# Block 0's attention fully by seven products, its matrix sums made earlier and sent through DRAM, and small steps reordered in a linear-attention + MLP kernel

## The chip, the cores and the metric

The kernel runs on one core of one Trainium2 chip. The metric is the time of one execution on the device in microseconds (us). Before the change it is 408.38 us, the median of three runs (408.17 to 408.54).

## The reference

```python
xn = layernorm(x)                                   # x: 2048 tokens x 512
qkv = xn @ wqkv                                     # 32 heads of 16
pq, pk = phi(q), phi(k)                             # phi(t) = (t+1 if t>0 else exp(t)) + 1e-6
kv = einsum("bhsd,bhse->bhde", pk, v); z = sum_s pk
o = (pq @ kv) / (pq . z + 1e-6)                     # per head
attention = o @ wo
h = relu(xn @ w1 + b1) ** 2                         # 512 -> 1376
out = x + attention + h @ w2 + b2
```

All is float32. What matters here: `kv` and `wo` are folded into one 512x512 matrix M, so that attention of a token is (weighted phi(q)) @ M.

## The kernel before, in words

**Precision.** Every matrix product is done on split numbers: a high part (float32r) and a low part (the rest). `three` (L130) and `PASSES` make one product from three matmuls: high*high, high*low, low*high. A split costs an ACT copy for the high part (`copy`, L114) and a DVE subtraction for the low part (`rest_of`, L125, or `split`, L122).

**Tiling.** 2048 tokens are four blocks of 512, and a block is four tiles of 128 tokens. A first stage normalises all tokens, makes keys and the matrix M; M's raw form goes to DRAM as `md`. Then a loop `for n in range(2)` takes the blocks in two pairs: blocks 3 and 2 (n=0), then blocks 1 and 0 (n=1). t1 is the first block of the pair, t2 the second.

**A pair's passes.** For each pair, passes p = 0 to 6 (NO = 7) make two 128-column chunks of q or of the MLP's hidden layer for both blocks at once, with Strassen's scheme: seven products of six matmuls instead of eight. Kinds by pass: q, w, q, w, w, w, w. They are written into four PSUM banks: A and `before` (banks 0 and 1, which change places from pass to pass), B (bank 2) and C (bank 3). On PE the order in a pass is: `A12`-type products into A and B, S1 into C, then the product `A22b` with `T[4]` into the bank `before` of the pass ahead, second-layer sums of the MLP (`mlp_2`, L501), then S2 into A, S4 into C, perhaps a second `mlp_2`, then S3 into A.

The product with `T[4]` is the place to watch. It adds onto the bank `before`, while that bank still holds the last pass's A, which is needed alone: at the start of the next pass DVE adds it to a saved value (L1184, `t5 = before + t5`). So PE cannot start the T[4] product until that DVE addition is done. In the trace this product is the second half of a row `b<-T,aop` of twelve matmuls, whose first half is S1. In names such as `t5_1_3`, `c12_1_3`, `c11_1_6` the first number is n and the second the pass that made it.

After the passes comes p = NO, a shorter one: `mlp_2`, the T[4] product, then block 1's attention by seven products (`Seven`), mixed with more `mlp_2`. Then block 0's MLP: nine `mlp_2` of twelve matmuls (e = 0 to 8), attention of block 0, the sums of the last two hidden chunks, and the stores.

**Seven.** `class Seven` (L972) does a block's attention product (512 tokens x 512) @ M by Winograd's seven quarter products instead of eight. It needs four sums over the block (`sums_o`, DVE, L986), four of M (`sums_m`), and the high and low parts of both sums (`parts_o`, `parts_m`). `run` (L1019, matmuls at L1028) issues six matmuls of 256 columns for one tile pair `e`; `into` (L1031, L1036) adds a PSUM half bank into the result in SBUF on DVE. `x` and `y` are the PSUM tiles that are shared by several quarters.

Before the change, block 1 goes through the full seven (both tile pairs, e = 0, 1). Block 0 uses `half = Seven(t2, (0,))` (L1476): tiles 0 and 2 by seven products, tiles 1 and 3 by `add_attention` (24 matmuls of 512 columns, L133). M is loaded again from `md` in pass 6 on SP's queue (`load_m`), its sums and parts are made by DVE and ACT in pass 6 and the pass after it.

**What sets the order.** Each engine executes its own instructions in the order in which the code issues them. Apart from the fixed order of the passes there are small steps of attention, queued in `steps[t1]` and `steps[t2]` (from `steps_of`, L421: phi, weighted, sums, quotients, divide, into_parts, for one of four chunks j of q). `step(k)` takes k of them out. Two hand-written tables say how many are taken where: `AT` (a row per pass, a column for each of nine places in the pass) and `AE` (one number for each e of block 0's MLP).

Of the kernel before, what the change touches and what calls it, by code (L numbers as in the profile page):

```python
# [18 lines left out]
def kernel(  # L19
# [401 lines left out]
    def steps_of(t, j, done=False, parts=False):  # L421


        o = q[t][:, j]
        tiles = []
        blocks = lambda ap: ap.rearrange("p (r c) -> p r c", c=32)
        heads_of = lambda ap: ap.rearrange("p (h d) -> p h d", h=H)
        by_heads = lambda ap: ap.rearrange("p (r h) d -> p r h d", h=2)

        def weighted():  # L430
            pz = w512(f"pz{t}_{j}", "p", 6)
            tiles.append(pz)
            nc.scalar.activation(pz, o, AF.Identity, bias=zc[:, 1, j:j + 1], scale=zc[:, 0, j:j + 1])

        def sums():
            pt = w512(f"pt{t}_{j}", "p", 6)
            den = small.tile([P, H], F32, name=f"dt{t}_{j}", tag="den")
            nc.vector.transpose(blocks(pt), blocks(tiles[0]))
            nc.vector.tensor_reduce(den, heads_of(pt), axis=AX.X, op=OP.add)  # L439
            tiles.append(den)  # L440

        def quotients():
            pz, den = tiles
            nc.vector.tensor_scalar(den, den, 1e-6, None, op0=OP.add)
            nc.vector.reciprocal(den, den)
            nc.vector.transpose(by_heads(heads_of(pz)), by_heads(den[:, :, None].to_broadcast([P, H, D // H])))

        def divide():
            nc.vector.scalar_tensor_tensor(o, o, 1e-6, tiles[0], op0=OP.add, op1=OP.mult)
# [519 lines left out]

    LO, HI = slice(0, D // 2), slice(D // 2, D)  # L970

    class Seven:  # L972
# [15 lines left out]
        def load_m(self):  # L988
            self.mt = both("mt", ("xs0h", "xs0l"))
            self.raw = four("mraw", "B0", pool=keep)  # L990
            nc.sync.dma_start(self.raw, md)
            self.m = [[self.raw[:, 2 * r:2 * r + 2, c] for c in (LO, HI)] for r in range(2)]

        def sums_m(self):

            (b11, b12), (b21, b22) = self.m
            return [lambda: self.op(b11, b12, b11, OP.subtract), lambda: self.op(b12, b22, b12, OP.subtract),
                    lambda: self.op(b22, b22, b11, OP.subtract), lambda: self.op(b21, b21, b22, OP.subtract)]
# [15 lines left out]

        def parts_m(self):

            return self.parts(self.raw, self.mt, ((1, HI), (0, HI), (0, LO), (1, LO)))
# [24 lines left out]
    for n in range(2):  # L1042
# [128 lines left out]
        for p in range(NO + 1):  # L1171
# [21 lines left out]
            if n and p == NO:  # L1193
                step()
                do(sums, 2)
                highs_m, lows_m = seven.parts_m()
            step(at_p[7] - (n and p == NO))
            if n and p == NO:
                do(highs_m, 2)
                do(sums)  # L1200
                do(highs_m, 2)
            if (kind, fa) == ("w", 2):
                next_2(2)
            if kind:
# [16 lines left out]
                step(at_p[0])  # L1221
            if kind:
# [36 lines left out]
            if n and p == NO - 1:  # L1259
                do(sums)  # L1260
                sums = seven.sums_m()
# [18 lines left out]
            if n and p == NO - 1:  # L1280
                do(sums)
            step(at_p[2])
            if p + 1 < NO:
# [9 lines left out]
            step(at_p[3])  # L1293
            if p == NO - 1 and n:
                do(bias, 2)
# [11 lines left out]
            step(at_p[4])  # L1307
            if n == 0 and p == 0:
# [11 lines left out]
            step(at_p[5])  # L1320
            if n and p == NO - 1:
# [16 lines left out]
            step(at_p[6])  # L1338
            if n == 0 and p == 0:
# [46 lines left out]
        if n:  # L1386
# [9 lines left out]
            do(lows_m, 4)  # L1396
# [46 lines left out]
        for e, f in enumerate(waiting[:-2]):  # L1443
            mlp_2(acc, f, s.pop(f))
# [43 lines left out]
        if n:  # L1488
            xh, yh = (bank(f"{w}h", "acc")[:, LO] for w in "xy")
            half.run(xh, ("a", 0, 0), ("m", 0, LO), 0, True)  # L1490
            half.run(acc[0][:, LO], ("a", 1, 0), ("m", 1, LO), 0)
            half.run(acc[2][:, LO], ("a", 1, 1), ("t", 1, LO), 0)
            half.into(xh, 0, LO)
            for f in reversed(last_two):
                wait_for(f)
            add_attention(acc, t2 * TB + 1)
            add_attention(acc, t2 * TB + last, True)
            half.run(acc[0][:, HI], ("s", 1, 0), ("m", 1, HI), 0)
            half.run(xh, ("s", 0, 0), ("t", 1, HI), 0)
            half.run(yh, ("s", 0, 1), ("t", 0, HI), 0, True)  # L1500
            half.into(xh, 2, LO)
            half.run(xh, ("s", 1, 1), ("t", 0, LO), 0)
            half.into(yh, 2, ALL)
            for k in (0, 2):
                half.into(xh, k, HI)
# [54 lines left out]
```

## Time and profile before

| what | before |
|---|---|
| median of three runs | 408.38 us |
| the profiled execution's own time | 408.15 us |
| its span on the core | 406.4 us |
| PE (matmuls) busy | 401.5 us, 99% of the span |
| DVE busy | 326.7 us, 80% |
| ACT busy | 274.0 us, 67% |
| POOL busy | 49.7 us, 12% |
| mean granted TensorE clock | 0.999 |

The profiled execution lies 1.75 us outside its span (start and end of the program) and 0.23 us below the median. A row of the timeline reads: start us, duration us, engine, line, operation, out<-in by the program's names without numbers, partitions x elements, count, and in brackets the engine's idle time just before with what ended it. A name like `b` or `t` stands for many tiles. PE's matmuls overlap, so the distance between starts tells their pace, not the duration. Second-pair passes start on PE at 253.7 (p=0), and block 0's attention at 387.5 us.

### The profile page before, as it was taken

Reading aid. Unit: us, or ns where it says so; the run is one execution under the profiler, and the core shown is the slowest. Engines: PE = TensorE matmul, PEld = TensorE weight load, DVE = VectorE, ACT = ScalarE, POOL = GpSimd, SP = SyncE. Lnnn points to the kernel's source line nnn. Section 1 sums busy time; section 2 is a strip of 40 time slices with the busy share of each in tenths; the row PEclk is TensorE's granted clock in tenths of the full one; section 3 lists DMA queues with packets and bytes.
Section 4 is the critical chain, followed back from the end, with each engine's and each line's share of the span. In section 5 each row is a group of like instructions: output and inputs, shape, how many; then the busy total and the mean of one; then the engine's idle time right before and its main releaser. Section 6 shows DMA issues by size and latency. Waiting matters only on the chain.

```text
span 406.4 us, 5813 instructions
## 1 busy us (share of the span) xinstructions
PE 401.5 (99%) x1993; PEld 333.1 (82%) x1993; DVE 326.7 (80%) x598; ACT 274.0 (67%) x478; POOL 49.7 (12%) x81
## 2 busy tenths in 40 slices
PE   8999999999999999999999999999999999999996
PEld 7788888888788888888878888888888888888885
DVE  5886667587898999988349997567989688999885
ACT  5677777556888788886818751677587859848440
POOL 5443333220000000030000300000000200000300
PEclk9999999999999999999999999999999999999999
DMA  5856657910563231381564912412221856015612
GB/s 213 278 168 223 208 158 205 257 29 0 130 184 80 77 103 27 105 214 19 202 232 131 209 33 101 118 53 52 52 79 32 229 103 232 2 52 202 110 26 103
DMA packets 47550, 51.10 MB, mean 126 GB/s; under 512 B 8417, under 2 KB 31201, under 8 KB 47138
## 3 DMA queue, kind: packets, MB, share of 16 engines
q1 hardware_dynamic: 45138, 46.55, 37.0%
q0 software_dynamic: 2304, 4.20, 6.4%
q8 instruction: 15, 0.25, 0.2%
q14 instruction: 13, 0.11, 0.1%
q10 hardware_dynamic: 80, 0.00, 0.0%
HBM read 38.81 MB, written 10.75 MB: 122 GB/s over the span
## 4 chain that ended last, share of the span: by engine, by line
PE 97%; DMA 1%; DVE 1%; ACT 0%; issue 0%
PE acc L133 33%; PE b L497 33%; PE pk L378 11%; PE kx L398 11%; PE acc L508 2%; PE acc L1028 2%; PE pz L133 1%; PE x L1028 1%; DMA x<-in_A_x_dram 1%; PE b L133 1%; PE pz0b L133 1%; PE xh L1028 1%; PE y L1028 0%; PE acc L515 0%; PE pt L310 0%; DVE st L236 0%
## 5 line engine op out<-in xcount | busy, mean ns | idle before, releaser
L133 PE MATMUL acc<-w2r,s 128*128 128x512 f32 x477 | 113.0, 390 | 0.0
L133 PEld LDWEIGHTS acc<-w2r,s 128*128 128x128 f32 x477 | 89.2, 188 | 19.1 <-issue 0.7
L497 PE MATMUL b<-T,aop 128*128 128x512 f32 x336 | 83.5, 389 | 0.0
L497 PEld LDWEIGHTS b<-T,aop 128*128 128x128 f32 x336 | 63.0, 188 | 13.9 <-ACT t L114 0.8
L1147 POOL DMA_DIRECT2D res<-in_B_b_dram x16 | 14.4, 1042 | 277.8 <-DVE dt L439 91.0
L398 PE MATMUL kx<-pk,tok 128*128 128x512 f32 x192 | 46.0, 389 | 0.0
L398 PEld LDWEIGHTS kx<-pk,tok 128*128 128x128 f32 x192 | 36.0, 188 | 7.6 <-ACT pk L114 0.2
L497 PE MATMUL b<-xs0h,aop 128*128 128x512 f32 x112 | 36.9, 390 | 0.0
L114 ACT ACTIVATE aop<-S 128x512 fp32r<-128x512 f32 x28 | 17.5, 624 | 12.5 <-DVE S L735 12.5
L359 POOL TENSOR_TENSOR tok<-xp,tok 128x512 fp32r<-128x512 f32 x15 | 20.2, 1344 | 39.7 <-ACT tok L114 39.7
L497 PEld LDWEIGHTS b<-xs0h,aop 128*128 128x128 f32 x112 | 21.0, 188 | 4.4
L125 DVE TENSOR_TENSOR w2r<-r,w2r 128x512 fp32r<-128x512 f32 (+2 forms) x35 | 23.7, 681 | 0.5 <-ACT w2r L114 0.4
L114 ACT ACTIVATE w2r<-r 128x512 fp32r<-128x512 f32 x32 | 19.6, 619 | 6.4 <-PE acc L133 5.5
L122 DVE TENSOR_TENSOR aop<-S,aop 128x512 fp32r<-128x512 f32 x28 | 19.2, 687 | 4.8 <-ACT aop L114 4.4
L497 PE MATMUL b<-xs0l,aop 128*128 128x512 f32 x56 | 21.8, 389 | 0.0
L133 PE MATMUL acc<-mh,aTsr 128*128 128x512 f32 x64 | 20.7, 389 | 0.0
L122 DVE TENSOR_TENSOR s<-c,s 128x512 fp32r<-128x512 f32 x20 | 13.5, 688 | 8.7 <-ACT s L114 8.6
L497 PE MATMUL b<-xs1h,aop 128*128 128x512 f32 x56 | 19.5, 389 | 0.0
L114 ACT ACTIVATE T<-Tf 128x512 fp32r<-128x512 f32 x16 | 9.5, 624 | 14.4 <-DVE Tf L678 14.3
L114 ACT ACTIVATE c<-b 128x512 f32<-128x512 f32 x28 | 16.4, 587 | 2.6 <-PE b L497 2.4
L369 ACT ACTIVATE k<-pk 128x512 f32<-128x512 f32 x16 | 9.4, 590 | 9.9 <-PE pk L378 9.8
L114 ACT ACTIVATE pk<-k 128x512 fp32r<-128x512 f32 x16 | 10.1, 631 | 8.6 <-DVE k L373 8.5
(259 smaller groups left out, 828.3 us busy)
## 6 DMA issues: line engine op xcount, KB each, us to landing
r<-in_B_w_dram SPq DMA_DIRECT2D x49, 256.0 KB, 3.5
res<-in_A_x_dram SPq DMA_DIRECT2D x8, 512.0 KB, 4.7
res<-in_B_b_dram POOLq DMA_DIRECT2D x16, 256.0 KB, 5.8
out_dram<-res SPq DMA_DIRECT2D x15, 256.0 KB, 2.2
via<-xp SPq DMA_DIRECT2D x5, 512.0 KB, 2.8
xg<-via SPq DMA_DIRECT2D x20, 128.0 KB, 2.8
xTd<-t SPq DMA_DIRECT2D x8, 256.0 KB, 4.1
x<-in_A_x_dram SPq DMA_DIRECT2D x4, 512.0 KB, 4.1
```

Source lines behind the costliest of these rows:

```text
L114: nc.scalar.activation(o, i, AF.Copy, bias=bias)
L122: ENG[el].tensor_tensor(out=l, in0=src, in1=f32(h), op=OP.subtract)
L125: nc.vector.tensor_tensor(out=l, in0=src, in1=f32(h), op=OP.subtract)
L133: nc.tensor.matmul(ps, lhsT=a[u], rhs=b[v], start=first and n == 0, stop=last and n == 2)
L359: ENG[el].tensor_tensor(out=l, in0=src, in1=f32(h), op=OP.subtract)
L369: nc.scalar.activation(p, ps, AF.Relu, scale=-1.0)
L378: nc.tensor.matmul(ps, lhsT=cols(i)[u][:, j, slot(i)], rhs=w[v][:, j, :], start=first and n == 0, stop=last and n == len(steps) - 1)
L398: nc.tensor.matmul(kxp[c], lhsT=tok[i][:, u, c * P:(c + 1) * P], rhs=pk[i][:, v], start=i == 0 and (u, v) == first, stop=i == NT - 1 and ( ...
L497: nc.tensor.matmul(ps, lhsT=a[u][:, j * P:(j + 1) * P], rhs=b[v][:, j, :], start=first and j == 0 and n == 0, stop=last and j == 1 and n == 2,
L508: nc.tensor.matmul(ps, lhsT=s[u][:, k * P:(k + 1) * P], rhs=w2s[NF - 1][u][:, a:z], start=first and u == 0, stop=stop and u == 1)
L1028: nc.tensor.matmul(ps, lhsT=a, rhs=b, start=first and i == 0 and n == 0, stop=False, skip_group_check=True)
L1147: nc.gpsimd.dma_start(r[:, i], b2[None, :].partition_broadcast(P), accum_op=OP.add)
```

## The change

Three things change, all for n = 1.

1. Block 0's attention goes through the full `Seven` (`half = Seven(t2)`): 84 matmuls of 256 columns in place of 42 of them and 24 of 512 columns. The last `mlp_2` before it (e = 8, hidden chunk 1) is moved behind it. For chunks j < 2 of blocks 0 and 1, only the half of the tokens that `Seven` reads is split (`into_parts`).
2. M's sums are made by a new function, `matrix_sums`: POOL's queue loads `md` into two tiles `mr0`, `mr1` at the start of n = 1; DVE makes four subtractions at place 0 of pass 1; four `parts` (an ACT copy into a tile `mh`, a DVE subtraction in place, and two POOL DMAs of 128x2x256 that store high and low parts to DRAM) are taken at places 5 and 6 of pass 1 and of pass 3. `load_m` then loads the finished parts on POOL's queue (two transfers of 1 MB) in pass 6, and the work on M in passes 6 and 7 is gone, as is SP's load of `md`.
3. The tables: `AT`'s last two rows, `AE`, and `step(3)` in place of the low parts of M take block 0's small steps earlier.

```diff
-            split(a[:, 0], a[:, 1], o, "act", "dve")
+            used = BT // 2 if t < NB // 2 and j < 2 else BT
+            split(a[:, 0, :used], a[:, 1, :used], o[:, :used], "act", "dve")
...
+    def matrix_sums():
+        t = [two(f"mr{r}") for r in range(2)]
+        for r in range(2):
+            nc.gpsimd.dma_start(t[r], md[:, 2 * r:2 * r + 2])
+        def op(o, x, y):
+            return lambda: nc.vector.tensor_tensor(out=o, in0=x, in1=y, op=OP.subtract)
+        def parts(r, at):
+            x, to = t[r][:, :, at], slice(2 * r, 2 * r + 2)
+            h = work.tile([P, 512], F32R, name=f"mh{r}{at.start}", tag="p", bufs=6).rearrange("p (j n) -> p j n", j=2)
+            copy("act", h, x)
+            rest_of(x.bitcast(F32R), x, h)
+            nc.gpsimd.dma_start(mtd[0][:, to, at], f32(h))
+            nc.gpsimd.dma_start(mtd[1][:, to, at], x)
...
-               (1, 0, 1, 0, 0, 0, 2, 0, 0),
-               (1, 0, 1, 0, 1, 1, 0, 2, 3)))[n]
+               (1, 0, 1, 1, 4, 0, 0, 0, 0),
+               (0, 0, 0, 0, 0, 0, 0, 4, 0)))[n]
...
-              (3, 2, 2, 3, 0, 5, 1, 6, 1, 5, 0))[n]
+              (2, 2, 2, 0, 0, 0, 0, 0, 0, 0, 0))[n]
+        TM = {(1, 0): 4, (1, 5): 1, (1, 6): 1, (3, 5): 1, (3, 6): 1} if n else {}
...
+            matrix_step(p, 5)
...
-            do(lows_m, 4)
+            step(3)
...
-                half = Seven(t2, (0,))
+                half = Seven(t2)
```

How rows move, first on ACT, at the turn from pass 1 to pass 2 of the second pair (`c12` and `t5` are the sums of pass 1, `aop` are split weights). Before:

```order
L485 ACTIVATE r2c1_2495<-c12_1_1_2688,b1s_97 128x512
L433 ACTIVATE pz1_0_2704<-q1_2509,zc_98 128x512
L114 ACTIVATE aop1_1_2414<-S3_2_2673 128x512
L485 ACTIVATE r2c1_2495<-t5_1_1_2639,b1s_97 128x512
L114 ACTIVATE c11_1_2_2726<-b1_0_2529 128x512
```

After:

```order
L486 ACTIVATE r2c1_2501<-c12_1_1_2698,b1s_97 128x512
L433 ACTIVATE pz1_0_2714<-q1_2515,zc_98 128x512
L114 ACTIVATE mh00_2716<-mr0_2495 128x512
L114 ACTIVATE mh0256_2721<-mr0_2495 128x512
L114 ACTIVATE aop1_1_2416<-S3_2_2683 128x512
L486 ACTIVATE r2c1_2501<-t5_1_1_2649,b1s_97 128x512
```

Two copies of the matrix sums have come in, behind `pz1_0`. On DVE at the same turn, before:

```order
L1311 TENSOR_TENSOR c12_1_1_2688<-b1_3_2532,c12_1_1_2688 128x512
L1184 TENSOR_TENSOR t5_1_1_2639<-b1_1_2530,t5_1_1_2639 128x512
L122 TENSOR_TENSOR aop1_1_2414<-S3_2_2673,aop1_1_2414 128x512
L438 STREAM_TRANSPOSE pt1_0_2722<-pz1_0_2704 128x512
L439 TENSOR_REDUCE dt1_0_2723<-pt1_0_2722 128x32
```

After:

```order
L1323 TENSOR_TENSOR c12_1_1_2698<-b1_3_2538,c12_1_1_2698 128x512
L125 TENSOR_TENSOR mr0_2495<-mr0_2495,mh00_2716 128x2x256
L125 TENSOR_TENSOR mr0_2495<-mr0_2495,mh0256_2721 128x2x256
L1203 TENSOR_TENSOR t5_1_1_2649<-b1_1_2536,t5_1_1_2649 128x512
L122 TENSOR_TENSOR aop1_1_2416<-S3_2_2683,aop1_1_2416 128x512
```

The two low parts now stand between `c12` and the `t5` addition, and each reads an `mh` that ACT must have copied first. At the turn from pass 3 to pass 4 the same happens with `mr1`: DVE's order becomes `c12_1_3`, low part, `w2r0`, low part, `t5_1_3`, and ACT's `mh1256`, `pz1_2`, `mh10` follow its relu of `c12_1_3`.

The third place is DVE from the end of pass 6 on (`s1_8` and `s1_9` are split hidden chunks, `pt`, `dt`, `pz` and `q0` belong to block 0's steps, `so1l` are low parts of block 1's sums). Before:

```order
L122 TENSOR_TENSOR s1_8_3244<-c11_1_6_3185,s1_8_3244 128x512
L986 TENSOR_TENSOR mraw_3214<-mraw_3214 128x2x256
L1311 TENSOR_TENSOR c12_1_6_3260<-b1_3_2532,c12_1_6_3260 128x512
L125 TENSOR_TENSOR w2r1_1021<-r2_9_3204,w2r1_1021 128x512
L438 STREAM_TRANSPOSE pt0_0_3290<-pz0_0_3248 128x512
L439 TENSOR_REDUCE dt0_0_3291<-pt0_0_3290 128x32
L444 TENSOR_SCALAR dt0_0_3291<-dt0_0_3291 128x32
L445 RECIPROCAL dt0_0_3291<-dt0_0_3291 128x32
L446 STREAM_TRANSPOSE pz0_0_3248<-dt0_0_3291 128x512
L1184 TENSOR_TENSOR t5_1_6_3216<-b1_0_2529,t5_1_6_3216 128x512
```

After, the same stretch:

```order
L122 TENSOR_TENSOR s1_8_3274<-c11_1_6_3215,s1_8_3274 128x512
L438 STREAM_TRANSPOSE pt0_0_3279<-pz0_0_3277 128x512
L439 TENSOR_REDUCE dt0_0_3280<-pt0_0_3279 128x32
L444 TENSOR_SCALAR dt0_0_3280<-dt0_0_3280 128x32
L445 RECIPROCAL dt0_0_3280<-dt0_0_3280 128x32
L446 STREAM_TRANSPOSE pz0_0_3277<-dt0_0_3280 128x512
L449 SCALAR_TENSOR_TENSOR q0_2516<-q0_2516,pz0_0_3277 128x512
L419 SCALAR_TENSOR_TENSOR q0_2516<-q0_2516,phi_3299 128x512
L1323 TENSOR_TENSOR c12_1_6_3293<-b1_3_2538,c12_1_6_3293 128x512
L125 TENSOR_TENSOR w2r1_1021<-r2_9_3234,w2r1_1021 128x512
L1203 TENSOR_TENSOR t5_1_6_3246<-b1_0_2535,t5_1_6_3246 128x512
```

Seven instructions of block 0's steps now stand ahead of `c12_1_6`, `w2r1` and `t5_1_6`. ACT's `w2r1` copy stands behind `pz0_1`, which reads what that `L419` row writes. Behind `t5_1_6` the same chain follows once more for the next chunk (`pt0_1` to `q0`, another seven), and only then `so1l` x4 and `s1_9`:

```order
L449 SCALAR_TENSOR_TENSOR q0_2516<-q0_2516,pz0_1_3303 128x512
L419 SCALAR_TENSOR_TENSOR q0_2516<-q0_2516,phi_3349 128x512
L125 TENSOR_TENSOR so1l_3315<-q1_2515,so1h_3314 128x2x256 x4
L122 TENSOR_TENSOR s1_9_3378<-c21_1_7_3371,s1_9_3378 128x512
L1050 TENSOR_TENSOR res1_0_3079<-x0_3392,res1_0_3079 128x256
```

Before, `so1l` stood behind one such chain and four sums of M.

More of the change, by code (lines that the diff above doesn't have):

```diff
@@ L989, in load_m @@
             self.mt = both("mt", ("xs0h", "xs0l"))
[L990 to L998, printed above, removed]
+            for o, src in zip(self.mt, mtd):
+                nc.gpsimd.dma_start(f32(o), src)
         def parts(self, src, to, order):
@@ L1192 @@
                 steps[t2] += steps_of(t2, pb)
[L1193 to L1201, printed above, removed]
+            step(at_p[7])
             if (kind, fa) == ("w", 2):
@@ L1260 @@
                 do(sums)
-                sums = seven.sums_m()
             if was == "w":
@@ L1279 @@
                 s[fa] = hidden_2(f"s{n}_{fa}", c11)
-            if n and p == NO - 1:
-                do(sums)
             step(at_p[2])
+            matrix_step(p, 2)
             if p + 1 < NO:
@@ L1443 @@
         for e, f in enumerate(waiting[:-2]):
-            mlp_2(acc, f, s.pop(f))
+            if n == 0 or e < NF - 3:
+                mlp_2(acc, f, s.pop(f))
             if e + 3 < NF - 2:
```

60 lines of the change are left out of this document (41 added, 19 removed).

## The prediction

> **What bounds the kernel now.** I read the page first: busy times, the granted clock, and the chain that ended last.
>
> ```profile
> span 406.4 us, 5813 instructions
> ...
> PE 401.5 (99%) x1993; PEld 333.1 (82%) x1993; DVE 326.7 (80%) x598; ACT 274.0 (67%) x478; POOL 49.7 (12%) x81
> ...
> PEclk9999999999999999999999999999999999999999
> ...
> PE 97%; DMA 1%; DVE 1%; ACT 0%; issue 0%
> ```
>
> PE is busy for 99% of the span at full clock, and the chain runs through PE for 97%. Next I read the waits, for PE alone.
>
> ```profile
> PE warm L528 <- PEq L1546: 0.8, 1, 0.8
> PE pt L310 <- DVE xp L600: 0.4, 1, 0.4
> ```
>
> These two, both near the start, are all that PE waits for in the list. So every matmul less shortens the kernel by its pace, and any new wait of PE lengthens it by its whole length, since there is no idle time later in which PE could win it back. Two questions follow: how many PE microseconds go, and whether DVE and ACT, which get the same work in other places, still deliver everything in time.
>
> **What PE saves.** The timeline of PE at the end, before, from the first matmul of block 0's attention to the first of the last sums:
>
> ```profile
> 387.50 0.28 PE L1028 MATMUL xh<-mh,aTsr 128*128 128x256 f32 x1
> ...
> 389.65 0.39 PE L133 MATMUL acc<-mh,aTsr 128*128 128x512 f32 x1
> ...
> 395.11 0.29 PE L1028 MATMUL acc<-mh,so0h 128*128 128x256 f32 x1
> ...
> 398.11 0.86 PE L133 MATMUL acc<-w2r,s 128*128 128x512 f32 x3
> ```
>
> The 24 wide matmuls of tiles 1 and 3 lie between 389.65 and 395.11: 5.46 us, 0.2275 us each. The whole takes 398.11 - 387.50 = 10.61 us. Block 1, which already goes through the full seven, gives the pace of the narrow ones:
>
> ```profile
> 349.36 0.28 PE L1028 MATMUL x<-mh,aTsr 128*128 128x256 f32 x1
> ...
> 353.66 2.91 PE L133 MATMUL acc<-w2r,s 128*128 128x512 f32 x12
> ```
>
> 36 matmuls in 4.30 us, 0.1194 us each, so a 256-column matmul costs more than half of a 512-column one. The 84 of the new form take 84 x 0.1194 = 10.03 us. The gain is 10.61 - 10.03 = **0.58 us**, and no more: the moved `mlp_2` costs the same behind the attention as before it.
>
> **First new wait: pass 1 to pass 2.** DVE, ACT and PE at that turn, before (`c` on L1311 is `c12_1_1`, `t` on L1184 is `t5_1_1`):
>
> ```profile
> 277.65 0.68 DVE L1311 TENSOR_TENSOR c<-b,c 128x512 f32<-128x512 f32 x1
> 278.25 0.68 DVE L1184 TENSOR_TENSOR t<-b,t 128x512 f32<-128x512 f32 x1
> ```
>
> ```profile
> 278.37 0.72 ACT L485 ACTIVATE r2c<-c,b1s 128x512 f32<-128x512 f32 x1 [1.36 <-DVE c L1311]
> 279.00 0.80 ACT L433 ACTIVATE pz<-q,zc 128x512 f32<-128x512 f32 x1
> 279.71 0.61 ACT L114 ACTIVATE aop<-S 128x512 fp32r<-128x512 f32 x1
> ```
>
> ```profile
> 278.61 2.91 PE L497 MATMUL b<-T,aop 128*128 128x512 f32 x12
> ```
>
> The T[4] product is the second six of that PE row: it starts at 278.61 + 6 x 0.2275 = 279.98. The addition it needs ends at 278.93, 1.05 us earlier. That is the whole cover. After the change two low parts stand ahead of the addition, and the second needs `mh0256`, the fourth ACT instruction counted from the relu at 278.37. Paces of copies and of low parts, from the sums of block 1:
>
> ```profile
> 343.23 2.18 ACT L114 ACTIVATE so1h<-q 128x512 fp32r<-128x512 f32 x4
> ...
> 349.63 2.49 DVE L125 TENSOR_TENSOR so1l<-q,so1h 128x512 fp32r<-128x512 f32 x4
> ```
>
> A copy takes 0.62 us, and the next starts 0.52 after it; a low part takes 0.69 and the next starts 0.60 after it. So `mh00` takes the place of the ACT row at 279.71 and ends at 280.33, `mh0256` ends at 279.71 + 0.52 + 0.62 = 280.85. DVE's low parts start at 280.37 and 280.97, the addition at 281.57, and it ends at 282.25. The end shows how long PE then needs:
>
> ```profile
> 396.76 0.42 DVE L1036 TENSOR_TENSOR res<-xh,res 128x256 f32<-128x256 f32 x1 [0.86 <-PE xh L1028]
> ...
> 397.33 0.36 PE L1028 MATMUL xh<-mth,so0h 128*128 128x256 f32 x1
> ```
>
> DVE ends at 397.18, the matmul that overwrites what it read starts at 397.33: 0.15 us. PE starts T[4] at 282.40 in place of 279.98: **2.42 us**. Behind the addition on DVE wait a low part of weights and the steps of block 1, whose users get the same 2.42 us more time. ACT's relu of `t5` waits with them.
>
> **Second: pass 3 to pass 4.**
>
> ```profile
> 301.27 0.68 DVE L1311 TENSOR_TENSOR c<-b,c 128x512 f32<-128x512 f32 x1
> ...
> 302.47 0.68 DVE L1184 TENSOR_TENSOR t<-b,t 128x512 f32<-128x512 f32 x1
> ```
>
> ```profile
> 301.99 0.72 ACT L485 ACTIVATE r2b<-c,b1s 128x512 f32<-128x512 f32 x1 [0.84 <-DVE c L1311]
> ```
>
> ```profile
> 303.12 2.88 PE L497 MATMUL b<-T,aop 128*128 128x512 f32 x12
> ```
>
> T[4] is due at 303.12 + 1.37 = 304.49. ACT: `mh1256` starts 0.63 after the relu (as 279.00 after 278.37), at 302.62, `pz1_2` at 303.14, `mh10` 0.71 later, at 303.85 to 304.47. DVE: the second low part at 304.51, the addition at 305.11 to 305.79, PE at 305.94: **1.45 us**. The clock times here are those of before; the first wait moves all three engines alike.
>
> **Third: pass 6 to the seven products.**
>
> ```profile
> 340.67 0.69 DVE L122 TENSOR_TENSOR s<-c,s 128x512 fp32r<-128x512 f32 x1 [0.49 <-ACT s L114]
> ...
> 343.09 0.70 DVE L438 STREAM_TRANSPOSE pt<-pz 128x512 f32<-128x512 f32 x1
> ...
> 345.15 0.71 DVE L446 STREAM_TRANSPOSE pz<-dt 128x512 f32<-128x512 f32 x1
> ...
> 346.36 0.67 DVE L449 SCALAR_TENSOR_TENSOR q<-q,pz 128x512 f32<-128x512 f32 x1
> ```
>
> ```profile
> 340.55 0.80 ACT L433 ACTIVATE pz<-q,zc 128x512 f32<-128x512 f32 x1
> ```
>
> ```profile
> 348.00 1.53 PE L497 MATMUL b<-T,aop 128*128 128x512 f32 x6
> ```
>
> The five instructions pt to pz take 345.86 - 343.09 = 2.77 us, since each needs the one before. After the change they start when ACT's pz ends, at 341.39, and end at 344.16. The division ends at 344.87, phi 0.60 later at 345.47. Only then can ACT start `pz0_1` (0.80), and the copy of `w2r1` behind it ends at 346.83; DVE has `c12_1_6` in between, but stands idle until that copy. Its low part ends at 347.55, `t5_1_6` at 348.15, and T[4] starts at 348.30: 0.30 us late. The next chain of five ends at 350.84, division 351.55, phi 352.15, the first `so1l` 352.75, the fourth 354.55, `s1_9` 355.15. PE comes to its first use of `so1l` at 349.66 + 26 x 0.1194 = 352.77 and waits until 352.90: 0.13. Ten matmuls later, at 354.09, begin those on `s1_9`; the third needs the low part, at 354.55, and gets it at 355.30: 0.75. Together **1.18 us**.
>
> **What I cost at nothing, and its cover.** The four sums of M in pass 1:
>
> ```profile
> 268.05 0.68 DVE L1210 TENSOR_TENSOR c<-b,c 128x512 f32<-128x512 f32 x1
> 271.55 0.69 DVE L419 SCALAR_TENSOR_TENSOR q<-b,phi 128x512 f32<-128x512 f32 x1 [2.82 <-ACT phi L418]
> ...
> 346.95 1.41 DVE L986 TENSOR_TENSOR mraw<-mraw 128x512 f32<-128x512 f32 x2
> ```
>
> Dependent ones cost 1.41 / 2 plus a few hundredths, four 2.9 us, against 2.82 us of idle DVE. They fit to within 0.1; without that hole they would push the turn of pass 1 by 2.9. Halved splits give back some tenths on engines that have them to spare. The parts load in pass 6 and are used a pass later. Block 0's wider sums and low parts (eight, at most 0.3 us more each) start earlier, because chunk 3's steps do; if that cover failed, up to 2.4 us would come on top. POOL's stores are weighed below.
>
> **The sum.** -0.58 + 2.42 + 1.45 + 1.18 = +4.47 us. On the profiled execution's 408.15 that is 412.6; on the median, 0.23 above it, 412.9. I forecast **412.9 us**, slower by 1.1%.
>
> **The rivals.** *POOL's stores hold ACT as well.* Freed `mh` buffers are awaited: `c12_1_4` on ACT in pass 4 waits for the store of `mh10`. POOL's rows:
>
> ```profile
> 321.48 2.65 POOL L1147 DMA_DIRECT2D res<-in_B_b_dram  x3 [90.96 <-DVE dt L439]
> 325.89 0.88 POOL L1147 DMA_DIRECT2D res<-in_B_b_dram  x1 [1.75 <-issue]
> ```
>
> ```profile
> out_dram<-res SPq DMA_DIRECT2D x15, 256.0 KB, 2.2
> ```
>
> The fourth transfer waits 1.75 us with nothing else to wait for, as if three of 128 rows were all that may be under way. The new stores have 256 rows each, so by that count one at a time. From 303.28 the third store begins two spacings later. With 4.41 us (325.89 - 321.48) it lands by 316.5, the copy ends at 317.1, and S3, due at 314.0 + 1.45, starts near 317.3: 1.8 us more, and some 0.5 in pass 2, where `pz1_1` waits for `mh0256`. With the 2.2 us of an SP store there is no wait. Price 0 to 2.3: 413 to 415.2. [...] No row shows such a store. Chance 0.18.
>
> *Only the first wait is real.* If ACT and DVE, given 2.4 us by PE's first wait, run ahead of it for the rest of the pair, the later waits are covered: 408.38 - 0.58 + 2.42 = 410.2. Against it: in passes 3 and 5 ACT waits for PE, so both start level again. Chance 0.12.
>
> *No wait at all: not slower.* One mechanism, at the first turn: the low parts fill holes on ACT (1.36 us idle before 278.37) and DVE. The price is then -0.58, 407.8. It decides at 279.83: the addition must end by then. For it speaks only that the holes exist; against it, that ACT reaches `mh00` behind a relu which itself waits for `c12`, so the copies stand after the hole, not in it. Chance 0.07.
>
> *The clock drops.* Should PE's 2.4 us of idleness halve the clock for the T[4] product and the twelve matmuls behind it, 18 x 0.2275 = 4.1 us come on top: 417. Every slice before shows full clock, and no idle time as long. [...] Chance 0.03.
>
> **How the numbers follow.** The forecast has 0.60. The range goes from 409.9, a little under the one-wait case, to 416.0, above the store case; it leaves out the no-wait and clock cases. About 0.2% (0.8 us) is what a measurement can tell here. The no-wait case, 0.14% faster, is mostly "same". Faster 0.02, same 0.05, slower 0.93.
>
> **What would show it.** In the changed profile PE's waits should have rows on DVE L1203, near 2.4 and 1.4 us, with idle time before `b<-T` at 280 and 307; a short one at 352, and one near 0.7 on `s1_9`. ACT's row for `mh0256` should end near 280.85. If `t5_1_1` ended before 279.8 the forecast fails. A PE wait in pass 4 before S3, ended by ACT `c`, would be the store rival.

## The result, and the profile after

| | before | after |
|---|---|---|
| median | 408.39 us (408.17 to 408.54, 5 runs) | 414.62 us (413.10 to 416.08, 5 runs) |
| ratio to before | | 1.0146 (95% interval 1.0116 to 1.0176) |
| the profiled execution's own time, its span | 408.15, 406.4 us | 414.62, 412.9 us |
| mean granted TensorE clock of the profiled execution | 0.999 | 0.996 |

The change makes the kernel slower by 6.2 us, where 4.5 were forecast. The five executions after the change lie in steps: 413.10 and 413.39 us with a mean clock of 1.000, 414.62 and 414.65 with 0.996, and 416.08 with 0.995. The first two are 4.7 and 5.0 us above before. What separates the others is the clock, which comes to light below.

PE's waits from 250 us on, after the change (engine, tile and line, the engine waited for, us in total, times, the longest). Before, this part of the list was empty:

```profile
PE b L498 <- DVE t L1203: 3.4, 2, 2.2
PE acc L133 <- DVE s L122: 0.5, 1, 0.5
```

This view counts from the end of the last matmul. By the starts of the matmuls, which are used below, each wait is some 0.16 us longer.

**The first turn**, pass 1 to pass 2, on DVE, ACT and PE (start, duration, engine, line, operation, tiles):

```profile
277.81 0.69 DVE L1323 TENSOR_TENSOR c<-b,c 128x512 f32<-128x512 f32 x1
280.51 1.29 DVE L125 TENSOR_TENSOR mr<-mr,mh 128x512 fp32r<-128x512 f32 x2 [2.02 <-ACT mh L114]
281.72 0.68 DVE L1203 TENSOR_TENSOR t<-b,t 128x512 f32<-128x512 f32 x1
```

```profile
278.53 0.72 ACT L486 ACTIVATE r2c<-c,b1s 128x512 f32<-128x512 f32 x1 [1.36 <-DVE c L1323]
279.15 0.80 ACT L433 ACTIVATE pz<-q,zc 128x512 f32<-128x512 f32 x1
279.86 1.14 ACT L114 ACTIVATE mh<-mr 128x512 fp32r<-128x512 f32 x2
```

```profile
278.76 1.52 PE L498 MATMUL b<-T,aop 128*128 128x512 f32 x6
282.46 2.44 PE L498 MATMUL b<-T,aop 128*128 128x512 f32 x6 [2.17 <-DVE t L1203]
```

DVE stands still for 2.02 us behind `c12`, until ACT has copied `mh00`; then come two low parts, then the addition, which ends at 282.40, and 0.06 later PE starts T[4]. It was due at 278.76 + 6 x 0.2275 = 280.13: 2.33 us late. But six matmuls of this product take 2.44 us, where the six above take 1.52. Some of that is the granted clock (window, its length, PE busy and instructions, clock, DMA share, GB/s):

```profile
280.20:282.40 2.20, 0.08 (x1) 1.00 0.09 32
282.40:284.50 2.10, 2.04 (x6) 0.66 0.84 276
284.50:286.40 1.90, 1.90 (x6) 0.50 1.03 301
286.40:288.00 1.60, 1.60 (x8) 0.98 0.14 56
```

A fall to one half that gives 0.66 over the second window lasts 2.10 x 0.34 / 0.5 = 1.43 us of it, so the clock stands at one half from about 283.1 to 286.4. The time lost is 2.10 x 0.34 + 1.90 x 0.50 = 1.66 us. The fall starts 0.6 us after PE has resumed, not with the wait.

**The second turn**, pass 3 to pass 4:

```profile
307.47 0.69 DVE L125 TENSOR_TENSOR mr<-mr,mh 128x512 fp32r<-128x512 f32 x1 [1.31 <-ACT mh L114]
...
308.70 0.69 DVE L125 TENSOR_TENSOR mr<-mr,mh 128x512 fp32r<-128x512 f32 x1
309.31 0.69 DVE L1203 TENSOR_TENSOR t<-b,t 128x512 f32<-128x512 f32 x1
```

```profile
307.32 1.52 PE L498 MATMUL b<-T,aop 128*128 128x512 f32 x6
310.05 1.65 PE L498 MATMUL b<-T,aop 128*128 128x512 f32 x6 [1.21 <-DVE t L1203]
```

Due at 307.32 + 1.365 = 308.69, started at 310.05: 1.37 us. Here the clock stays at full speed, yet these six matmuls take 0.13 us longer than those ahead of them: at the four restarts on wide matmuls in this trace (282.46, 310.05, 353.95 and 360.98) the second matmul starts 0.34 us after the first, 0.11 more than the pace of 0.2275. So each of these waits is counted with 0.11 on top of its length.

**The third place**, DVE and PE from pass 6 to the seven products:

```profile
353.21 0.68 DVE L1203 TENSOR_TENSOR t<-b,t 128x512 f32<-128x512 f32 x1
...
357.83 2.49 DVE L125 TENSOR_TENSOR so1l<-q,so1h 128x512 fp32r<-128x512 f32 x4
360.24 0.69 DVE L122 TENSOR_TENSOR s<-c,s 128x512 fp32r<-128x512 f32 x1
```

```profile
350.98 2.88 PE L133 MATMUL acc<-w2r,s 128*128 128x512 f32 x12
353.95 1.66 PE L498 MATMUL b<-T,aop 128*128 128x512 f32 x6
...
359.86 0.63 PE L133 MATMUL acc<-w2r,s 128*128 128x512 f32 x2
360.98 1.20 PE L133 MATMUL acc<-w2r,s 128*128 128x512 f32 x4 [0.50 <-DVE s L122]
```

T[4] is due at 350.98 + 12 x 0.2275 = 353.71 and starts 0.24 late; the matmul that needs the low part of `s1_9` is due at 360.31 and starts 0.67 late. Between them the starts of the narrow matmuls show 0.11 more at the first use of `so1l`, where the view of the waits has none.

**The attention of block 0** starts and ends its 84 matmuls as forecast, 391.76 to 401.79, 10.03 us:

```profile
391.76 0.28 PE L1042 MATMUL xl<-mh,aTsr 128*128 128x256 f32 x1
...
401.67 0.28 PE L1042 MATMUL xl<-mth,so0l 128*128 128x256 f32 x1
401.79 3.59 PE L133 MATMUL acc<-w2r,s 128*128 128x512 f32 x15
```

**The sum by what was measured**, profiled execution against profiled execution: -0.58 (attention), +2.44 and +1.48 (the two turns, with the 0.11), +1.24 (third place: 0.24 + 0.11, 0.11, 0.67 + 0.11), +1.66 (clock) give +6.24 us. The difference of the two is 414.62 - 408.15 = 6.47. Of the rest of 0.23, 0.15 lies ahead of the first turn (278.76 against 278.61); the last 0.08 is not accounted for.

### The profile page after: what moved, and what is told of

It is laid out like the page before. It is cut to its first block, busy times and chain, and to the rows that moved or that the text cites. A ratio compares the mean times of both kernels' runs of the same rounds, so it can differ in the third digit from the quotient of the medians.

```text
span 412.9 us, 5889 instructions
## 1 busy us (share of the span) xinstructions
PE 404.1 (98%) x2011; PEld 334.8 (81%) x2011; DVE 329.5 (80%) x603; ACT 273.6 (66%) x478; POOL 57.6 (14%) x93
## 4 chain that ended last, share of the span: by engine, by line
PE 84%; DVE 7%; ACT 5%; issue 1%; DMA 1%; SPq 0%; DVEq 0%; ACTq 0%
PE acc L133 28%; PE b L498 25%; PE pk L378 11%; PE kx L398 11%; PE acc L509 2%; PE acc L1042 1%; PE pz L133 1%; DMA rk<-in_A_wqkv_dram 1%; PE xl L1042 1%; DVE q L419 1%; DVE aop L122 1%; DVE S L736 1%; PE x L1042 1%; PE b L133 1%; PE pz0b L133 1%
## 5 line engine op out<-in xcount | busy, mean ns | idle before, releaser
L133 PE MATMUL acc<-w2r,s 128*128 128x512 f32 x477 | 114.2, 392 | 0.5 <-DVE s L122 0.5
L498 PE MATMUL b<-T,aop 128*128 128x512 f32 x336 | 85.0, 393 | 3.5 <-DVE t L1203 3.4
L1174 DVE TENSOR_TENSOR res<-acc,res 128x512 f32<-128x512 f32 x16 | 10.5, 688 | 7.9 <-PE acc L133 5.1
L433 ACT ACTIVATE pz<-q,zc 128x512 f32<-128x512 f32 x16 | 12.9, 808 | 5.7 <-DVE q L419 5.7
```

Of the source, the lines that this page charges most:

```text
L133: nc.tensor.matmul(ps, lhsT=a[u], rhs=b[v], start=first and n == 0, stop=last and n == 2)
L498: nc.tensor.matmul(ps, lhsT=a[u][:, j * P:(j + 1) * P], rhs=b[v][:, j, :], start=first and j == 0 and n == 0, stop=last and j == 1 and n == 2,
L1174: nc.vector.tensor_tensor(out=r[:, a:z], in0=ps, in1=r[:, a:z], op=OP.add)
```

## The experiments

Five rounds each beside the kernel before, whose median was 408.2 to 408.5 us in every group, except the two on the clock with three. Waits of PE are differences of its matmuls' starts from the pace.

### e1_behind: the four parts behind the t5 addition

```diff
-        TM = {(1, 0): 4, (1, 5): 1, (1, 6): 1, (3, 5): 1, (3, 6): 1} if n else {}
+        TM = {(1, 0): 4, (2, 7): 2, (4, 7): 2} if n else {}
...
+            matrix_step(p, 7)
             step(at_p[7])
```

> The four parts of M's sums (copy, low part, two stores each) are issued right behind the t5 addition of the next pass and its relu, not ahead of it; nothing else differs from the changed kernel. My theory: both long PE waits (2.3 and 1.4 us before the T[4] product) go and with them the fall of the clock, while the attention's saving (0.58) and the waits behind pass 6 (about 1.2) stay: 408.4 - 0.58 + 1.2 = 409.0 us, 408.8 to 409.4, clock 1.000 in every execution. Rival one, the work itself is too much for DVE and ACT in these passes: the same microseconds come back as a wait at another row, 411 to 413. Rival two, the clock falls for another reason than the first wait (the new POOL transfers, say): clock 0.996 in about half the executions and some 1.6 us more in those.

Measured 410.57 us (410.21 to 412.37), ratio 1.0061 (1.0045 to 1.0077). Both long waits are gone, but 1.5 us more is left than I expected. PE's waits:

```profile
PE b L498 <- ACT c L114: 0.6, 1, 0.6
PE acc L133 <- DVE s L122: 0.5, 1, 0.5
PE b L498 <- DVE t L1203: 0.4, 1, 0.4
```

The first line is a new wait of 0.80 us at 288.46, ahead of S3 in pass 2. ACT's row for it reads:

```profile
285.08 0.69 ACT L486 ACTIVATE c<-b,b1s 128x512 f32<-128x512 f32 x1 [1.28 <-DVE dt L439]
```

ACT's relu of `c21` waits 1.28 us for DVE's `dt`, which now stands behind the two low parts; everything behind it on ACT, the copy of `c12` too, is late. The wait at the T[4] product behind pass 6 has grown as well, from 0.24 to 0.57 us (the third line). With the new wait's restart of 0.11 the two make 1.2 of the 1.5 us; the rest is not accounted for. So rival one was half right: the work can be put elsewhere for less, not for nothing. As to the clock, five executions have 0.998 to 1.000, and one, at 412.37 us, 0.996; it has no trace.

### e2_early_copies: ACT's copies earlier, low parts where they were

`parts` is split in two, `high` (ACT's copy) and `low` (DVE's subtraction and the stores). The copies of passes 1 and 3 are issued at place 3, ahead of the S2 product; the low parts stay ahead of the addition.

```diff
-        TM = {(1, 0): 4, (1, 5): 1, (1, 6): 1, (3, 5): 1, (3, 6): 1} if n else {}
+        TM = {(1, 0): 4, (1, 3): 2, (1, 5): 1, (1, 6): 1, (3, 3): 2, (3, 5): 1, (3, 6): 1} if n else {}
```

> The ACT copies of M's sums are issued before the S2 product of passes 1 and 3, the low parts on DVE stay ahead of the t5 addition. It asks how much of the first two waits is DVE's two extra instructions and how much is that they stand still for ACT's late copies. My theory: the low parts no longer wait, so DVE's addition comes 1.2 us later than before the change at the first turn, against 1.05 us of cover: PE waits 0.1 to 0.5 us there and 0 to 0.2 at the second; the waits behind pass 6 stay at 1.2: 409.1 to 409.8 us, clock 1.000. Rival, that two more instructions ahead of the addition cost their time in full, whoever copies: 2 x 0.6 at each turn, 408.4 - 0.58 + 1.2 + 2.4 = 411.4. Second rival, the copies stand ahead of the c12 copy on ACT and only move the lateness there: a wait of over 1 us at the first turn remains, over 410.5.

Measured 409.76 us (409.56 to 410.14), ratio 1.0037 (1.0025 to 1.0049), clock 0.999 to 1.000. DVE at the first turn:

```profile
277.91 0.68 DVE L1328 TENSOR_TENSOR c<-b,c 128x512 f32<-128x512 f32 x1
278.51 1.29 DVE L125 TENSOR_TENSOR mr<-mr,mh 128x512 fp32r<-128x512 f32 x2
279.71 0.69 DVE L1208 TENSOR_TENSOR t<-b,t 128x512 f32<-128x512 f32 x1
```

The same two instructions stand ahead of the addition without idle time, and PE does not wait there at all, nor at the second turn. So the two long waits were those for ACT's copies. In their place 0.58 + 0.11 us come ahead of S3 of pass 1, since the `c12` copy now stands behind the early copies: the second rival, in small.

### e6_second_only: the first turn alone relieved

The first two copies stand behind the phi step of pass 1, where ACT is idle; the rest is as in the change (a copy and a low part together count two in pass 3, since `parts` is split as in e2).

```diff
-        TM = {(1, 0): 4, (1, 5): 1, (1, 6): 1, (3, 5): 1, (3, 6): 1} if n else {}
+        TM = {(1, 0): 4, (1, 4): 2, (1, 5): 1, (1, 6): 1, (3, 5): 2, (3, 6): 2} if n else {}
```

> The changed kernel with the first two ACT copies of M's sums issued behind the c12 copy and the phi step of pass 1, in the 1.36 us for which ACT stands idle there; the second two and everything else as in the change. My theory: the first wait goes to at most 0.3 us and takes the fall of the clock with it, the second (1.4 and 0.1 to start again) and the waits behind pass 6 (1.2) stay: 408.4 - 0.6 + 0.2 + 1.5 + 1.2 = 410.7 us, 410.4 to 411.1, clock 1.000 in every execution. Rival, a wait of 1.4 us is enough to bring the clock down now and then: some executions at 0.996 and 1.6 us longer.

Measured 410.95 us (410.74 to 411.68), ratio 1.0065 (1.0052 to 1.0077), clock 0.999 or 1.000 in all six executions. The waits are 0.21 + 0.11 at the first turn, 1.37 + 0.11 at the second, 1.25 behind pass 6. The fall of the clock is gone with the first wait, and the second, of 1.37 us, was not followed by one in any of the six.

### e3_old_order and e5_attention_only: the full seven without the early steps

e3 is the changed kernel with the tables of before:

```diff
-               (1, 0, 1, 1, 4, 0, 0, 0, 0),
-               (0, 0, 0, 0, 0, 0, 0, 4, 0)))[n]
+               (1, 0, 1, 0, 0, 0, 2, 0, 0),
+               (1, 0, 1, 0, 1, 1, 0, 2, 3)))[n]
...
-              (2, 2, 2, 0, 0, 0, 0, 0, 0, 0, 0))[n]
+              (3, 2, 2, 3, 0, 5, 1, 6, 1, 5, 0))[n]
...
-            step(3)
```

e5 is the kernel before with the new order of products at the end and nothing else:

```diff
-            mlp_2(acc, f, s.pop(f))
+            if n == 0 or e < NF - 3:
+                mlp_2(acc, f, s.pop(f))
...
-                half = Seven(t2, (0,))
+                half = Seven(t2)
...
```

> The changed kernel with the order of the small steps of before (last two rows of AT, AE, no three steps in place of the low parts of M). My theory: of the three waits only the third goes (1.2 us, behind pass 6); the first two and the fall of the clock in about half the executions stay: 413.2 - 1.2 = 412.0 us where the clock holds, 413.5 where it falls. Rival, the waits behind pass 6 come from the loads of M's parts and POOL's transfers, not from the order of the steps: they stay, 413.1 to 414.7 as before.

> The kernel before with one part of the change: block 0's attention by the full seven products and the last mlp_2 behind it; M's sums and the order of the steps as before. My theory: 84 narrow matmuls in place of 42 and 24 wide ones save 0.58 us, and block 0's wider sums and low parts are covered: 407.8 us, 407.6 to 408.1. Rival, the doubled sums and low parts of block 0 come late without the reordered steps: a wait of up to 2.4 us at the first use of their results, up to 410.2.

Measured: e3 420.11 us (419.06 to 420.97), ratio 1.0288 (1.0270 to 1.0305); e5 416.68 us (415.30 to 416.94), ratio 1.0198 (1.0183 to 1.0212). Both expectations were far off. PE's waits in e5:

```profile
PE xl L1028 <- DVE res L1036: 2.8, 1, 2.8
PE acc L1028 <- ACT so0h L114: 1.1, 1, 1.1
...
PE acc L1028 <- ACT aTsr L114: 0.8, 1, 0.8
```

All are in block 0's attention. Its sums and low parts are twice as wide now, and with the old order DVE comes to them too late: its four sums run from 388.39 and its low parts from 391.96, where PE has reached the products that need them at 391.98 - 1.21 = 390.77. In the changed kernel they run from 385.87 and 389.44, and PE needs them at 396.06. The waits add up to 6.5 us with their restarts, and the clock falls as well, here under narrow matmuls (window, its length, busy time and instructions of PE, weight loads, DVE, ACT and POOL, the granted clock, DMA share, GB/s):

```profile
394.00:397.00 3.00, 0.20 (x3) 0.06 (x1) 2.94 (x6) 2.20 (x5) 0.00 (x0) 0.80 0.40 87
397.00:402.40 5.40, 5.40 (x25) 5.40 (x26) 2.38 (x5) 0.00 (x0) 0.00 (x0) 0.50 0.00 0
402.40:405.00 2.60, 2.60 (x19) 2.38 (x18) 2.37 (x6) 0.00 (x0) 0.00 (x0) 0.96 0.00 0
```

Half the clock under 24 matmuls at 0.2135 us in place of 0.1194 costs 2.3 us. 6.5 + 2.3 - 0.58 is 8.2 of the 8.3 us measured. In e3 the third wait behind pass 6 is gone, as expected, and the waits of the first two turns stay at 2.31 and 1.37. So the early steps are not a part of the change that could be left out: they buy the seven products their sums, at the price of 1.2 us behind pass 6.

### e7_delay45 and e7_delay67: from which wait does the clock fall?

```diff
+            for _ in range((5, 4)[p % 2] if was else 0):
+                nc.vector.tensor_tensor(out=t5, in0=t5, in1=t5, op=OP.max)
             if was:
                 nc.vector.tensor_tensor(out=t5 if was == "w" else q[t2][:, pb], in0=before, in1=t5, op=OP.add)
```

> The kernel before with extra DVE work ahead of each t5 addition (the maximum of t5 with itself, which leaves it as it is): four times in the even passes, five in the odd ones, 0.6 us each, in both pairs. PE then waits before each T[4] product some 2.4 - 1.05 = 1.35 or 3.0 - 1.05 = 1.95 us; 14 turns in an execution. It asks from which length of a wait the clock falls. [...] Rival two, any wait of over 1 us can: falls at the 1.35 turns too.

> The same with six extra DVE instructions in the even passes and seven in the odd ones: waits of some 2.55 and 3.15 us. [...]

The expectations have the passes the wrong way round: `(5, 4)[p % 2]` gives five in the even ones and four in the odd, and seven and six in the other kernel. Nor are the waits 1.35, 1.95 and so on, since the cover differs from turn to turn; what counts is each turn's wait, as the traces show it. Measured 448.57 us (clock 0.976 to 0.980) and 472.92 us (0.953 to 0.960). All PE waits over 0.9 us from 100 us on in both, and the longer ones of the changed kernel and e3:

| PE's wait, us | times | the clock fell after it |
|---|---|---|
| 0.97 to 2.02 | 8, and 1.37 in each of the other two | never |
| 2.31 to 2.76 | 3 at 2.47, 2.51, 2.64; one at 2.75; 2.31 (e3) and 2.33 (after) | all but that of 2.75 |
| 2.96 to 3.35 | 3.09, 3.10, 3.14, 3.35; 2.96 (e3) | all but that of 3.14 |
| 3.46 to 5.33 | 9 | always |

Most falls are one stretch of 3.41 us at half the clock. Two turns of e7_delay45, at 135.23 and at 308.31, in PE's rows and, with the same columns as for e5, in the granted clock:

```profile
135.23 1.78 PE L497 MATMUL b<-T,aop 128*128 128x512 f32 x6 [2.94 <-DVE t L1186]
136.81 4.42 PE L133 MATMUL acc<-w2r,s 128*128 128x512 f32 x12
...
308.31 1.66 PE L497 MATMUL b<-T,aop 128*128 128x512 f32 x6 [2.58 <-DVE t L1186]
309.81 2.90 PE L133 MATMUL acc<-w2r,s 128*128 128x512 f32 x12
```

```profile
135.20:136.40 1.20, 1.17 (x5) 0.99 (x6) 1.13 (x4) 1.19 (x3) 0.00 (x0) 1.00 0.07 14
136.40:139.80 3.40, 3.40 (x11) 2.59 (x10) 2.42 (x5) 3.13 (x7) 0.00 (x0) 0.53 0.30 80
...
308.30:311.70 3.40, 3.38 (x15) 2.79 (x16) 3.30 (x7) 3.26 (x6) 0.00 (x0) 1.00 0.29 77
```

After the first, PE runs 1.4 us at full clock before the fall; after the second, none comes. By the granted clock, the slow stretches of e7_delay45 end at 122.95, 140.02, 170.74, 204.87, 341.40 and 375.54 us, and these are 5, 9, 10, 40 and 10 times 3.413 us apart, to within 0.02 ((375.54 - 122.95) / 74 = 3.413). The traces show the granted clock, not what sets it. What follows is a tally by a ruler of my own, bins of 3.413 us laid end to end through the ends of a trace's slow stretches, with every wait split at their edges. The wait before 135.23 in e7_delay45 and the one of 3.14 us before 227.52 in e7_delay67, in bins laid so (bin, its length, PE busy and instructions, granted clock, DMA share, GB/s):

```profile
133.19:136.60 3.41, 1.37 (x6) 1.00 0.03 5
136.60:140.02 3.42, 3.42 (x10) 0.50 0.30 79
...
222.92:226.34 3.42, 1.62 (x8) 1.00 0.00 0
226.34:229.75 3.41, 2.23 (x10) 1.00 0.00 0
```

The first wait has 1.06 us ahead of the edge at 133.19 and 2.04 behind it; the clock fell where that second bin ends, at 136.60. The wait of 3.14 has 1.95 and 1.18 us in its two bins, that of 2.75 has 1.70 and 1.04, and no fall followed. Each fall in these two traces came behind a bin with at least 2.04 us of waiting, and the largest amount in a bin without a fall behind it is 1.95. In e5 the clock fell at 395.80, in the middle of a wait, behind a bin with 0.32 us of one wait and 1.79 of the next. It then stayed down for 6.8 us, two bins, as it did twice in e7_delay67; in these three the wait reached 1.1 to 1.6 us into the first slow bin. The rival of a fall after any wait of over 1 us is out: none of those of 0.97 to 2.02 was followed by one. Nor does length alone sort the waits: 2.75 and 3.14 us brought no fall, 2.31 to 2.64 did.

For the five executions of the changed kernel this gives an estimate, from the bins of 3.41 us, the wait of 2.33 and the 1.95 and 2.04 above: if the wait falls anywhere in the bins with equal chance, and the clock falls where some 2.0 us of it lie in one, that is so in (3.41 + 2.33 - 2 x 2.0) / 3.41, about one half, of the executions; 3 of 5 were seen with a clock of 0.996 or less. Only one of the five has a trace; in it the whole wait, 280.13 to 282.46, lies in the bin that ends at 283.06, where the clock fell.

### e8 to e12: can the third wait be avoided for nothing?

All five have M's copies early, as above. They differ in where block 0's steps stand: how many at place 4 of pass 6, ahead of `so1l`, behind `s1_9`, behind the last sum into block 1's result, and at e = 0, 1, 2 of block 0's MLP (the change: 4, 4, 3, 0 and 2, 2, 2). The edit of e9, of which the others are variants:

```diff
-               (1, 0, 1, 1, 4, 0, 0, 0, 0),
-               (0, 0, 0, 0, 0, 0, 0, 4, 0)))[n]
+               (1, 0, 1, 1, 3, 0, 0, 0, 0),
+               (0, 0, 0, 0, 0, 0, 0, 0, 0)))[n]
...
-              (2, 2, 2, 0, 0, 0, 0, 0, 0, 0, 0))[n]
-        TM = {(1, 0): 4, (1, 5): 1, (1, 6): 1, (3, 5): 1, (3, 6): 1} if n else {}
+              (3, 2, 2, 0, 0, 0, 0, 0, 0, 0, 0))[n]
+        TM = {(1, 0): 4, (1, 4): 2, (1, 5): 1, (2, 7): 1, (3, 3): 2, (3, 5): 1, (3, 6): 1} if n else {}
...
+            matrix_step(p, 7)
             step(at_p[7])
...
-            step(3)
+            step(7)
```

In e8 both low parts of pass 1 stay ahead of the addition (`(1, 5): 1, (1, 6): 1`). The places of the steps:

| kernel | place 4, ahead of so1l, behind s1_9, behind the sums | e = 0, 1, 2 |
|---|---|---|
| e8_no_waits | 3, 4, 3, 0 | 3, 2, 2 |
| e9_steps_behind | 3, 0, 7, 0 | 3, 2, 2 |
| e10_steps_later | 3, 0, 4, 0 | 5, 3, 2 |
| e11_steps_split | 3, 0, 4, 3 | 3, 2, 2 |
| e12_steps_filled | 3, 0, 4, 2 | 4, 2, 2 |

> The changed kernel with all three waits taken away by order alone: the ACT copies of M's sums earlier (pass 1 in ACT's idle stretch behind the phi step, pass 3 before the S2 product), and one of block 0's small steps handed out later (three in place of four at place 4 of pass 6, three in place of two at e = 0 of block 0's MLP). My theory: the three waits are the whole loss, so what is left is the 0.58 us that the attention saves: 408.4 - 0.58 = 407.8 us, 407.6 to 408.2, clock 1.000. Rival, the earlier steps are late wherever they stand between pass 6 and the seven products, and the shift only moves the wait: 408.8 to 409.2. Second rival, the copies of pass 1 come late behind the phi step and hold the low parts: 0.5 us more.

> All three waits taken away in another manner than in e8_no_waits, which had a wait of 2.0 us in front of so1l instead: the four small steps of block 0 that stand between the t5 addition after pass 6 and so1l are handed out behind so1l and s1_9 (seven steps there in place of three), place 4 of pass 6 hands out three in place of four, and e = 0 three in place of two. M's copies in pass 1 are as in e8_no_waits, with one low part ahead of the t5 addition and one behind it. My theory, that each wait is only a matter of what stands ahead of what: no wait is left, 408.2 - 0.58 = 407.6 to 408.0 us, clock 1.000. Rival, block 0's steps are then late for its own MLP or its sums, since DVE has no idle time from 360 to 388 us in the changed kernel: a wait of 1 to 3 us at the sums' parts of block 0, 409 to 411. Second rival, the low part behind t5 holds a buffer that the relu of c21 waits for, as both did in e1_behind: some 0.3 to 0.5 us more.

> The same, but the displaced steps are spread further: four behind s1_9 in place of three, and five, three and two at e = 0, 1, 2 of block 0's MLP. My theory: as e9_steps_behind, 407.6 to 408.0 us, since ACT's and DVE's work is the same and four microseconds lie between block 0's low parts of sums and their first use. Rival: steps spread later make the parts of block 0 late as in the old order, 409 to 412; if this kernel is slower than e9_steps_behind, lateness is what counts, and the change's early order is needed for the full seven products.

> e9_steps_behind with three of the seven steps moved once more, from ahead of the sums into block 1's result to behind the last of them. In e9_steps_behind PE waited 1.0 us for a PSUM half bank that those sums had not yet read, and some 0.6 us more a little later; in e10_steps_later these waits were gone, but the steps came too late for block 0 (0.8 + 0.5 us at w2r parts, 1.0 at a bank of block 0's attention). My theory, that each of these is a matter of order alone: here neither is left, 408.4 - 0.58 = 407.8 us, 407.6 to 408.3. Rival, DVE has no room left between 360 and 388 us: one of the two groups of waits stays, 409 to 410.3.

> e11_steps_split with two steps in place of three behind the last sum into block 1's result, the third (its transpose had DVE stand idle 0.88 us for ACT) going to e = 0 of block 0's MLP, where other work stands between. In e11_steps_split one wait is left, 0.97 us for a bank of block 0's attention, since DVE comes to the sum out of that bank 0.8 us late. My theory: the 0.88 us of idle DVE pass on to that sum, so the wait goes to about 0.1: 408.4 - 0.58 + 0.1 + 0.3 (what e11_steps_split has more than its waits account for) = 408.2 us, 408.0 to 408.5, no longer to be told from the kernel before. Rival, the step at e = 0 makes a later w2r part late, as in e10_steps_later: 408.7 to 409.3.

| kernel | median, us | ratio (95%) | PE's waits from 250 us on, with their restarts |
|---|---|---|---|
| e8 | 411.93 | 1.0087 (1.0075 to 1.0099) | 2.1 at so1l, 0.8 at s1_9, 0.3 at the first turn |
| e9 | 410.01 | 1.0036 (1.0024 to 1.0049) | 1.1 for block 1's bank x, 0.5 behind it |
| e10 | 410.30 | 1.0049 (1.0036 to 1.0063) | 0.5 and 0.8 at w2r parts, 1.0 for bank xl |
| e11 | 409.20 | 1.0015 (0.9996 to 1.0034) | 1.0 for bank xl |
| e12 | 410.38 | 1.0056 (1.0042 to 1.0070) | 0.5 and 0.8 at w2r parts, 1.0 for bank xl |

The theory expected 407.6 to 408.5 us of these five and missed each time; the rival's range held in e9 (with the waits at another place than it named), e10 and e11, and e8 and e12 lie above theirs. In e9 to e12 nothing waits any more at t5, so1l or s1_9: the third wait was a matter of order. But each time DVE is late somewhere else. In e8 moving one step put `pz` on ACT behind the four copies of `so1h`, and DVE waited for it:

```profile
351.17 0.71 DVE L438 STREAM_TRANSPOSE pt<-pz 128x512 f32<-128x512 f32 x1 [2.99 <-ACT pz L433]
```

e12, meant to fill 0.88 us of idle DVE, opened a hole of 2.07 (`s<-r2a`, for ACT), and its rival's mechanism came true at more than its price (410.38 us against 408.7 to 409.3). e11 has one wait left:

```profile
391.84 0.36 PE L1047 MATMUL xl<-mth,so0h 128*128 128x256 f32 x1 [0.81 <-DVE res L1055]
```

The interval of e11 takes in 1, but only through one execution of the kernel before at 412.34 us (clock 0.992): its other 14 lie at 407.99 to 408.68, and all eleven of e11 at 408.85 to 409.78. So e11 is slower as well, by some 0.8 us. None of the twelve kernels beats it; the 0.58 us to be had are smaller than what each rearrangement gave back.

## Why the prediction was right, and where it was off

Forecast 412.9 us, range 409.9 to 416.0; measured 414.62. Point by point:

- **PE saves 0.58 us.** Right: 10.03 us for the 84 matmuls. No run shows the gain by itself, since e5 brought waits with it.
- **First wait, 2.42 us.** Measured 2.33 + 0.11. The mechanism is the one named: the copies stand on ACT behind a relu that needs `c12`, the low parts on DVE wait for the copies, the addition for the low parts. e2 shows it from the other side.
- **Second wait, 1.45 us.** Measured 1.37 + 0.11; it is not covered by the first, against the second rival (one wait, 410.2). e6 shows it alone.
- **Third wait, 1.18 us** in parts of 0.30, 0.13 and 0.75. Measured 0.35, 0.11 and 0.78. That these come from the order of the steps is shown by e9 to e12, that they could be avoided for nothing is not.
- **Costed at nothing.** Block 0's wider sums and low parts were covered by the early steps, as forecast. The price without that cover was mis-sized: up to 2.4 us by my text, 8.3 by e5, for I counted the longer instructions and not that PE waits at five places, for 5.9 us and the restarts, and that the clock falls.
- **POOL's stores.** The rival is out. The first three of each four follow one another without a pause, all eight land 2.6 to 3.7 us after their issue, where the rival had 4.41, and ACT's copy of `c12_1_4` at 317.55 has no idle time ahead of it:

```profile
307.85 0.71 POOL L989 DMA_DIRECT2D mthd<-mh  x1 [23.31 <-ACT mh L114]
308.57 0.72 POOL L990 DMA_DIRECT2D mtld<-mr  x1
309.29 0.71 POOL L989 DMA_DIRECT2D mthd<-mh  x1
```

- **The clock.** Here a rival with a chance of 0.03 came true in 3 of 5 executions. Its size was wrong as well: I let the clock fall for the T[4] product and twelve matmuls behind it, 4.1 us, and in the trace it fell for 3.41 us, at a cost of 1.66. Without it the sum stands where it was forecast: 413.10 and 413.39 against 412.9. That the median of 414.62 still lies in the range is in part luck: the range left the clock case out, and its upper end of 416.0 was set by the store case, which did not come. One execution, at 416.08, lies above it. The argument "every slice before shows full clock, and no idle time as long" said only that such a wait was not in the trace.

## What to carry to other kernels

On a kernel whose busiest engine never waits, look for every place where moved work stands ahead of an instruction that this engine waits for, and add up the queue there: who must finish before whom, on which engine. The amount of the work says little (at the first turn the two low parts cost nothing when their copies were early, and 2.3 us when they were late), and a second engine that stands still in the middle of its queue was the costliest form here (DVE idle for 2.02 us at the first turn, for 2.99 in e8). The long waits also put PE's clock at risk: of the 20 waits of 2.31 us and more in the table of e7, 18 were followed by a fall of the clock to one half, of the ten up to 2.02 us none. Such a fall cost 1.66 us by the trace of the changed kernel, 1.4 us between its executions at 0.996 and those at 1.000, and 2.3 us in e5, where it lasted 6.8 us; that came on top of the wait's length.

## What the runs showed of the hardware that I had not expected

- The granted clock fell to one half after the wait of 2.33 us in the changed kernel, for 3.41 us from 283.06, at a cost of 1.66 us, and after 18 of the 20 waits of 2.31 us and more in the table of e7, this one among them. The ends of the slow stretches of e7_delay45 lie whole multiples of 3.413 us apart, to within 0.02. In e5 and twice in e7_delay67, where the wait reached 1.1 us or more into the slow stretch, the clock stayed down for two such lengths (6.8 us in e5).
- PE lost 0.11 us more at each restart on wide matmuls in the changed kernel, at the second matmul (0.34 us behind the first, the pace being 0.2275), and some 0.08 us in e11 on narrow ones (0.20 against 0.1194).
- What stays open: the one execution at 416.08 us (clock 0.995), 1.4 us above those with one fall; that of e1 at 412.37; and one of the 59 of the kernel before, at 412.34 us with a clock of 0.992, where the longest wait of PE in the kernel's profile is 0.8 us. None of them has a trace. Nor have the two executions of e8 with a clock of 0.996; its longest wait is 1.99 us, between the largest sum in a bin of e7 without a fall, 1.95, and the smallest with one, 2.04.
